# Layer norm by a scaled 16-point matrix in the first stage of a spectral block and feed-forward kernel, on one core

## The chip, the cores and the metric

The kernel runs on one core of one Trainium2 chip. A core has five engines with instruction queues of their own: TensorE (PE in the profile; PEld is its weight loads), VectorE (DVE), ScalarE (ACT), GpSimd (POOL) and SyncE (SP). SP, ACT and POOL also issue the transfers (DMAs). The metric is the device time of one launch in microseconds.

## The reference

x has 2048 rows (tokens) of 448 elements in bf16. Twice over, a spectral block and a feed-forward block are added to it:

```python
x = x + A(layernorm(x), w_r, w_i)      # A: irfft2( rfft2(x) * (w_r + 1j*w_i) ) over tokens and elements
x = x + B(layernorm(x), w1, b1, w2, b2) # B: relu(x @ w1 + b1)**2 @ w2 + b2, inner width 1792
x = x + A(layernorm(x), w_r, w_i)
x = x + B(layernorm(x), w1, b1, w2, b2)
```

The layer norm takes mean and variance of each token's 448 elements and has no weights: (x - mean) / sqrt(var + 1e-5). Both layers use the same weights.

## The kernel before

**Tiling.** x is held as 16 tiles t of 128 partitions by 448 elements; partition p of tile t is token 16p + t. The transform over the 2048 tokens is done as a 16-point one across groups of partitions and a 128-point one behind it; that over the 448 elements is a matrix product (called the d-transform here) with sine and cosine tables that use the symmetry of x[d] and x[447 - d].

**First stage.** For each tile, `ln_stats` gets mean and 1/sqrt(var + eps) (VectorE's batch-norm instructions and ScalarE's root, or for tiles 1 and 3 ScalarE's accumulating square and copy), `norm` (L676) writes the normalised tile into `x_sb`, on GpSimd for 12 tiles and on VectorE for four, and `first_A` multiplies it with the 128x256 matrix `FA_sb` (the 16-point matrix spread over the partitions, and its negative beside it). The normalised tile is the stationary operand, in four matmuls per tile. They leave the sum and the difference of the two halves of the tile, transformed over 16 points, in one bank of PSUM. ScalarE evicts that bank into `XA` (L656). In XA, tiles 0 to 7 take the even columns of the second token index, and tiles 8 to 15 the odd ones, so the d-transform of one half can run when eight tiles are in.

**Spectral block.** Then follow, for each of eight pairs of 16-point outputs: `stage_TD` (d-transform, tables `TD_sb`), `stage_B` (128-point transform, `G_sb`), `stage_W` (the product with w_r and w_i, on VectorE; the weights lie in `Wt`, a half of them copied into reversed order by GpSimd, L657, from two gathered transfers), `stage_Bi` (128-point inverse, `H_sb` and `HS_sb`). `stage_TI` and `stage_AI` go back to elements and tokens.

**Feed-forward block.** `ln_B` squares on ScalarE and sends the tile transposed into `yT`, by matmuls for the first two tiles and by transposing DMAs for the others. `h_part` and `h_pairs` make the inner layer for four tiles at a time, `o_tile` the outer one. In layer 1 each finished tile goes straight into the second spectral block's first stage, `second_A`, which scales `FA_sb` by the tile's 1/deviation (`scaled`, L668) into one of the `NFS` buffers of `Fs`, on VectorE, and uses it as moving operand.

**What sets the order.** Operations are grouped into units, and `ORDER` gives every unit a rank, by tag and place in it ("A1.4" is the first stage for tiles 4 and 5; the letters a, d, p put a unit on ScalarE, VectorE or GpSimd). `ranked` sorts by these, and each engine runs its instructions in that order. `schedule` goes through the sorted units with a cost for each operation. It gives out the eight PSUM banks, and where it expects TensorE to be idle, it puts in matmuls of ones that keep it busy. `emit` puts the waits on semaphores. A queue never looks past an instruction that waits, and SP's queue issues its transfers in rank order as well. Transfers of x go out first, in five pieces:

```python
for i, (a, b) in enumerate(((0, 2), (2, 4), (4, 8), (8, 12), (12, 16))):
    dma("act" if i in (1, 3) else "sp", xin[:, a:b, :], x_dram[:, a:b, :])
```

By the ranks of these five, SP sends tiles 0 to 1, then 12 to 15, then 4 to 7; ACT sends 8 to 11, then 2 and 3, and then FA. On GpSimd, x_sb's padding is zeroed (0.94 us) between the first and second normalisation, and 13 of the 14 copies into `Wt` come after the last one.

Of the kernel before, what the change touches and what calls it, by code (L numbers as in the profile page):

```python
# [15 lines left out]
NFS = 6  # L16
# [6 lines left out]
NB = 8  # L23
# [18 lines left out]
def make_constants():  # L42
# [75 lines left out]
    for g, M in enumerate((cl * np.cos(th), cl * np.sin(th))):  # L118
# [201 lines left out]
class _Sched:  # L320
# [5 lines left out]
    NDSEM = {"sp": 20, "pool": 16, "act": 8, "pe": 0, "dve": 0}  # L326
    DMA_RATE = 400.0
    TURN = (200.0, 100.0)
    SLACK = 40.0
    DMA_SLACK = 100.0  # L330
    BEGIN = 800.0
    WINDOW = 3413.0
# [1051 lines left out]
```

## Time and profile before

| what | value |
|---|---|
| median of three runs | 285.54 us (285.1 to 286.15) |
| the profiled execution | 285.39 us, with a span of 283.6 us from the first instruction to the last |
| TensorE busy, of the span | 263.4 us (93%) |
| VectorE, ScalarE | 209.7 us (74%), 177.9 us (63%) |
| GpSimd | 30.1 us (11%) |
| mean granted TensorE clock | 0.976 |
| moved by DMA | 18.05 MB |

A line of a group reads: line of the kernel, engine, operation, output <- inputs, shapes, count, then busy time in us and the mean of one in ns, then idle time of the engine just before, and what ended most of it. A line of a timeline begins with start and busy length in us. The busy time of matmuls is modelled: their starts are exact, their ends overlap. Many operations are issued by helpers, so a line number is that of the helper: L631 is every matmul, L656 and L657 are evictions and copies on ScalarE and the other engines, L623 every plain transfer.

### The profile page before, as it was taken

To read this page: it belongs to the slowest core of one execution; us is meant where nothing else is said; L and a number is where in the kernel's file an instruction comes from. 1 tells how busy PE (TensorE), PEld (TensorE's weight loads), DVE (VectorE), ACT (ScalarE), POOL (GpSimd) and SP (SyncE) were. 2 spreads that over 40 slices of the span, in tenths; PEclk is the share of its full clock that TensorE was granted. 3 is DMA by queue.
4 is the path that set the end of the run, shared out by engine and by line. 5 is a ranking of instruction groups with operands and counts; after the bars stand their busy time and mean duration, and the time that the engine had idled before them with its cause. 6 is when DMAs were issued, how large, how long until landed. Compare 5 with 4: busy or idle time off the path is not lost.

```text
span 283.6 us, 5727 instructions
## 1 busy us (share of the span) xinstructions
PE 263.4 (93%) x2154; PEld 160.4 (57%) x2156; DVE 209.7 (74%) x669; ACT 177.9 (63%) x389; POOL 30.1 (11%) x35
## 2 busy tenths in 40 slices
PE   7347898999998999999999999999999999999996
PEld 2123666568954455445556876478854454576554
DVE  4643299949968897879699999968879785254732
ACT  3544789789870575778532989598961870987100
POOL 3999900000000000000000000000000000000000
PEclk9875999999999999999999999999999999999999
DMA  7996940001023013230000000002031305400032
GB/s 255 364 361 203 280 168 0 2 0 33 7 40 69 2 37 66 39 38 2 0 2 0 3 2 2 0 0 42 2 75 32 55 0 91 81 10 0 3 113 65
DMA packets 27007, 18.05 MB, mean 64 GB/s; under 512 B 20034, under 2 KB 25378, under 8 KB 26852
## 3 DMA queue, kind: packets, MB, share of 16 engines
q1 hardware_dynamic: 26260, 15.10, 21.0%
q0 software_dynamic: 288, 1.84, 1.7%
q10 hardware_dynamic: 432, 0.75, 0.8%
q8 instruction: 17, 0.28, 0.4%
q14 instruction: 10, 0.08, 0.1%
HBM read 12.18 MB, written 1.84 MB: 49 GB/s over the span
## 4 chain that ended last, share of the span: by engine, by line
PE 81%; POOL 5%; DMA 5%; ACT 4%; DVE 3%; issue 1%; SPq 0%; ACTq 0%; DVEq 0%
PE ps L631 81%; POOL x_sb L676 5%; DMA xin<-in_A_x_dram 3%; ACT arena L656 2%; DMA yT<-arena 2%; ACT tmp L656 1%; DVE st L785 1%; DVE arena L683 1%; DVE x_sb L1084 0%; ACT VT L1108 0%; SPq L623 0%; DVE tmp L683 0%; ACT mv L650 0%; DVE x_sb L1204 0%; DVE mv L776 0%
## 5 line engine op out<-in xcount | busy, mean ns | idle before, releaser
L631 PE MATMUL ps<-yT,W_sb 64*128 64x512 bf16 (+1 forms) x770 | 90.1, 346 | 0.0
L631 PE MATMUL ps<-W_sb,arena 128*128 128x448 bf16 (+1 forms) x476 | 87.8, 342 | 1.2 <-DVE arena L683 1.2
L631 PEld LDWEIGHTS ps<-yT,W_sb 64*128 64x128 bf16 (+1 forms) x770 | 53.4, 95 | 33.9 <-issue 1.5
L650 ACT ACTIVATE arena<-ps,b1col 128x512 bf16<-128x512 f32 x84 | 52.0, 689 | 28.0 <-PE ps L631 27.9
L631 PEld LDWEIGHTS ps<-W_sb,arena 128*128 128x128 bf16 x476 | 45.8, 98 | 38.7 <-DVE arena L683 3.0
L683 DVE TENSOR_TENSOR arena<-arena 128x512 bf16<-128x512 bf16 (+1 forms) x140 | 44.5, 363 | 14.6 <-ACT arena L650 14.5
L656 ACT ACTIVATE XA<-ps 128x512 bf16<-128x512 f32 x32 | 21.9, 743 | 19.4 <-PE ps L631 19.3
L656 ACT ACTIVATE arena<-ps 128x448 bf16<-128x448 f32 (+1 forms) x41 | 24.7, 725 | 3.8 <-PE ps L631 3.6
L1204 DVE SCALAR_TENSOR_TENSOR x_sb<-ps,arena 128x448 bf16<-128x448 f32 (+1 forms) x26 | 15.0, 582 | 13.4 <-PE ps L631 13.2
L1108 ACT ACTIVATE VT<-x_sb 128x448 bf16<-128x448 bf16 x32 | 18.6, 588 | 9.4 <-DVE x_sb L1084 9.4
L631 PE MATMUL ps<-FA_sb,x_sb 128*128 128x256 bf16 x64 | 12.6, 353 | 12.4 <-POOL x_sb L676 7.2
L676 POOL TENSOR_SCALAR x_sb<-xin,mv,rstd 128x448 bf16<-128x448 bf16 x12 | 22.1, 1850 | 3.4 <-DVE rstd L792 3.4
L650 ACT ACTIVATE mv<-mv,epst 128x1 f32<-128x1 f32 (+1 forms) x44 | 12.1, 295 | 12.0 <-DVE mv L786 10.9
L650 ACT ACTIVATE arena<-ps 128x256 bf16<-128x256 f32 x56 | 17.9, 408 | 2.3 <-PE ps L631 2.3
L631 PEld LDWEIGHTS ps<-FA_sb,x_sb 128*128 128x128 bf16 x64 | 6.6, 118 | 18.5 <-POOL x_sb L676 11.3
L656 ACT ACTIVATE VT<-ps 128x512 bf16<-128x512 f32 (+1 forms) x28 | 13.8, 556 | 4.9 <-PE ps L631 4.7
L631 PE MATMUL ps<-yT,VT 64*128 64x512 bf16 x42 | 15.8, 376 | 0.0
L656 ACT ACTIVATE tmp<-ps 128x896 bf16<-128x896 f32 (+1 forms) x20 | 14.4, 793 | 1.2 <-PE ps L631 1.2
L631 PE MATMUL ps<-arena,G_sb 128*128 128x448 bf16 (+1 forms) x76 | 14.5, 333 | 0.7 <-ACT arena L656 0.5
L631 PE MATMUL ps<-HS_sb,arena 128*128 128x512 bf16 x62 | 14.4, 379 | 0.1
L631 PE MATMUL ps<-TD_sb,XA 112*64 112x112 bf16 (+2 forms) x296 | 13.8, 223 | 0.0
L1084 DVE SCALAR_TENSOR_TENSOR x_sb<-ps,mv,xin 128x448 bf16<-128x448 f32 x16 | 10.4, 677 | 4.2 <-PE ps L631 4.2
(71 smaller groups left out, 297.2 us busy)
## 6 DMA issues: line engine op xcount, KB each, us to landing
out_dram<-x_sb SPq DMA_DIRECT2D x15, 112.0 KB, 2.0
W_sb<-in_B_w_dram SPq DMA_DIRECT2D x1, 1568.0 KB, 11.7
W_sb<-in_B_w_dram SPq DMA_DIRECT2D x1, 1344.0 KB, 6.7
HS_sb<-c_HS SPq DMA_DIRECT2D x1, 1024.0 KB, 6.7
G_sb<-c_G SPq DMA_DIRECT2D x1, 960.0 KB, 13.4
xin<-in_A_x_dram SPq DMA_DIRECT2D x2, 448.0 KB, 6.0
xin<-in_A_x_dram ACTq DMA_DIRECT2D x1, 448.0 KB, 4.6
Wt<-in_A_w_r_dram SPq DMA_DIRECT2D x1, 392.0 KB, 14.0
```

The source lines that it names most:

```text
L631: return sch.add("pe", lambda e: e.matmul(_res(o), lhsT, rhs, start=start, stop=stop, skip_group_check=skip), [lhsT, rhs], [o], cost=cost, ...
L650: sch.add("act", lambda e: e.activation(o, _res(i), func, **kw), rd, [o], cost=c)
L656: op = sch.add(engs[0], lambda e: e.activation(o, _res(i), ACT.Copy) if h[0].eng == "act" else e.tensor_copy(o, _res(i)), [i], [o], cost=c ...
L676: op = sch.add(engs[0], lambda e: e.tensor_scalar(o, i, m, r, op0=ALU.subtract, op1=ALU.mult), [i, m, r], [o], cost=c[engs[0]])
L683: sch.add(eng, lambda e: e.tensor_tensor(o, _res(a), b, op), [a, b], [o], cost=_free(o) / rate + 69.0)
L785: small(lambda e, si=si, xi=xi: e.bn_stats(si, xi), [xi], [si], (c1 - c0) / 0.96 + 69.0)
L1084: small(lambda e, xx=xx, xi=xi, r=r, m=m: e.scalar_tensor_tensor(out=xx, in0=_res(r), scalar=m, in1=xi, op0=ALU.subtract, op1=ALU.add), [r ...
L1108: sch.add("act", lambda e, i=i, o=o, x=x: e.activation(o, x, ACT.Square, accum_out=mv[:, i, 4:5]), [x], [o, mv[:, i, 4:5]], cost=560.0)
L1204: small(lambda e: e.scalar_tensor_tensor(out=o, in0=_res(i), scalar=r[0] if r else 1.0, in1=xb[:, t, d0:d1], op0=ALU.mult, op1=ALU.add), [ ...
```

## The change

The tile is not normalised any more. For each tile, `scaled` writes 1/deviation times `FA_sb` (both halves, 128x256) into one of four `Fs` buffers, and the raw tile from `xin` is the stationary operand of the same four matmuls. The mean is taken off in a fifth matmul: `minus` puts -2 x mean (a mean for each half of the tile) into `m2`, in bf16, and a column of it, broadcast to 128 columns, is the stationary operand; the scaled matrix is the moving one, and the result is added to the sums. 13 of the scalings are on GpSimd, those of tiles 8, 14 and 15 on VectorE. x's tiles 0 to 3 come in a transfer each. The feed-forward of the last tile ends in three pieces of columns and not in two. Every unit has a new rank. The planner's margins are larger, and it reckons 1900 ns more for the transposing DMA of tiles 4 and 5 in layer 1.

```diff
-NFS = 6
+NFS = 4
+NORM1 = ()
...
-    SLACK = 40.0
-    DMA_SLACK = 100.0
+    SLACK = 60.0
+    DMA_SLACK = 200.0
...
-        Fs = sb("Fs", [P, NFS, P])
+        Fs = sb("Fs", [P, NFS, 2 * P])
+        m2 = sb("m2", [P, 2, NT])
...
-        for i, (a, b) in enumerate(((0, 2), (2, 4), (4, 8), (8, 12), (12, 16))):
-            dma("act" if i in (1, 3) else "sp", xin[:, a:b, :], x_dram[:, a:b, :])
+        for a, b in ((0, 1), (1, 2), (2, 3), (3, 4), (4, 8), (8, 12), (12, 16)):
+            dma("act" if a in (1, 3, 8) else "sp", xin[:, a:b, :], x_dram[:, a:b, :])
...
+        def minus(a, b):
+            o, i = m2[:, 0, a:b], mv[:, a:b, 0:1].to_broadcast([P, b - a, 2])
+
+            def twice(e):
+                with nc.allow_low_precision(reason="two equal terms"):
+                    return e.tensor_reduce(o, i, mybir.AxisListType.X, ALU.add, negate=True)
+
+            small(twice, [mv[:, a:b, 0]], [o])
...
         def first_A(t):
 
-            xh, m, r = x_sb[:, t, 0:D], mv[:, t, 0:1], rstd[:, t, 0:1]
-            norm(xh, xin[:, t, :], m, r, EV["XH"])
             q = _Tile(1)
-            F2 = FA_sb[:, None, 0:P].to_broadcast([P, 2, P])
+            m, r = mv[:, t, 0:1], rstd[:, t, 0:1]
+            own = t in NORM1
+            if own:
+                x, f = x_sb[:, t, 0:D], FA_sb
+                norm(x, xin[:, t, :], m, r, EV["XN1"])
+            else:
+                x, f = xin[:, t, :], Fs[:, t % NFS, :]
+                scaled(f, FA_sb[:], r, EV["FS"])
+            F2 = f[:, None, 0:P].to_broadcast([P, 2, P])
...
             for k in range(2):
-                mm(o(k), x_sb[:, t, D0[k]:D0[k] + P], F2, k == 0, False, skip=True)
-                mm(o(k), x_sb[:, t, HD + D0[k]:HD + D0[k] + P], FA_sb[:], False, k == 1, skip=True)
+                mm(o(k), x[:, D0[k]:D0[k] + P], F2, k == 0, False, skip=True)
+                mm(o(k), x[:, HD + D0[k]:HD + D0[k] + P], f[:, 0:2 * P], False, own and k == 1, skip=True)
+            if not own:
+                mm(q[lambda b: ps[:, b, :].rearrange("p (k g c) -> p k g c", k=2, g=2)[:, :, 0, :]],
+                   m2[:, 0, t:t + 1].to_broadcast([P, P]), F2, False, True, skip=True)
             A_out(t, q, EV["A1"])
...
-                for d0, d1 in (CUT if t == NT - 1 else ((0, D),)):
+                for d0, d1 in ((0, D),) if t < NT - 1 else CUT_OUT if last else CUT:
...
             ln_stats(g, xin, 0, on_act)
+            minus(g[0], g[-1] + 1)
             for t in g:
                 first_A(t)
```

The ranks of the first stage, and of what is transferred and copied beside it (a unit's number is its place in the order of all engines; in "A1.t" the statistics come first, and the last three of each tile are scaling, matmuls, eviction):

```diff
-    "A1.0": "7 8 11 17 42p 45 48"
-    "A1.2": "83 94 106 131 137d 140 146"
-    "A1.4": "56 75 55 76 85 86 93d 105 108 98p 135 136"
...
+    "sp.xin": "6 4 7 16", "act.xin": "3 10 12", "act.FA_sb": "11"
+    "sp.Wt": "18 17 244 85", "sp.TD_sb": "28", "sp.G_sb": "37 112", "sp.W1_sb": "84 290 291 292", "sp.HS_sb": "111",
+    "sp.TI_sb": "116", "sp.H_sb": "120 119", "sp.b2row": "121", "sp.J_sb": "153", "sp.W2_sb": "288", "pool.x_sb": "183"
+    "A1.0": "9 25 26 30 46 63p 64 65", "A1.1": "13 14 24 23 27 39 43 57 71p 72 78", "A1.2": "8 19 20 32 44 60p 61 62"
+    "A1.3": "38 40 52 41 45 48 49 55 73p 80 81", "A1.4": "31 42 29 33 51 53 56 74p 82 91 77p 93 95"
+    "A1.6": "47 54 34 50 66 67 70 79p 96 104 92p 105 106", "A1.8": "58 68 59 69 83 86 90 89d 107 109 101p 122 128"
+    "A1.10": "75 87 76 88 97 98 100 113p 127 129 123p 130 139"
+    "A1.12": "99 103 94 102 110 114 131 125p 138 143 140p 141 144"
+    "A1.14": "115 118 108 117 132 133 135 136d 145 154 134d 142 151"
+    "TD0.0": "146 148d 155 156a", "TD0.1": "147 149d 157 159a", "TD0.2": "126 137d 158 160d"
+    "M.0": "150 124", "M.1": "187 184", "M.2": "211 152", "M.3": "220 221", "M.4": "248 210"
```

More of the change, by code (lines that the diff above doesn't have):

```diff
@@ L377, in add @@
             u = self.new_unit(eng)
+        if not u.tag:
+            u.tag = f"{eng}.{writes[0].tensor.name}" if writes else eng
         if tile is not None and tile.unit is None:
@@ L477, in schedule @@
                             break
-                        b = min((bank_free[b], b) for b in range(NB) if b not in taken and (
-                            bank_user[b] is None or all(x in done for x in bank_user[b].readers)))
+                        b = min(((bank_free[b], b) for b in range(NB) if b not in taken and (
+                            bank_user[b] is None or all(x in done for x in bank_user[b].readers))), default=None)
+                        if b is None:
+                            break
                         if b[0] > f:
@@ L618, in dma @@
                 fn = lambda e: e.dma_start_transpose(o, i)
-                sch.add(eng, fn, reads, writes, is_dma=True, cost=1000.0, lat=300.0)
+                sch.add(eng, fn, reads, writes, is_dma=True, cost=1000.0, lat=lat)
             else:
@@ L1127, in ln_B @@
                 dma("sp", yT[:, t:t + n, :, :].rearrange("p t k c -> p (t k) c"),
-                    xn[:, 0:n, :].rearrange("p t c -> p (t c)"), transpose=True)
+                    xn[:, 0:n, :].rearrange("p t c -> p (t c)"), transpose=True, lat=1900.0 if t == 4 and not last else 300.0)
             sch.tag = "xb" + sch.tag
@@ L1218, in second_A @@
             A_out(t, q, EV["A2"])
+        CUT_OUT = ((0, HD), (HD, HD + QD), (HD + QD, D))
         CUT = ((0, HD), (HD, D)) if HALVES else ((0, D),)
```

4 lines of the change are left out of this document (2 added, 2 removed), and 187 rows, old and new, of the table ORDER.

## The prediction

> **What bounds the kernel now.** I first read the page's totals and slices: TensorE carries most of the span, and GpSimd's work all lies in the first eighth.
>
> ```profile
> span 283.6 us, 5727 instructions
> PE 263.4 (93%) x2154; PEld 160.4 (57%) x2156; DVE 209.7 (74%) x669; ACT 177.9 (63%) x389; POOL 30.1 (11%) x35
> POOL 3999900000000000000000000000000000000000
> PEclk9875999999999999999999999999999999999999
> L676 POOL TENSOR_SCALAR x_sb<-xin,mv,rstd 128x448 bf16<-128x448 bf16 x12 | 22.1, 1850 | 3.4 <-DVE rstd L792 3.4
> ```
>
> Then the chain of waits in order of time (start, length, what). Up to 30.8 us it runs mostly through GpSimd's normalisations of x (L676).
>
> ```profile
> 1.66 9.08 DMA xin<-in_A_x_dram
> ...
> 17.55 6.13 POOL x_sb L676 x4
> ...
> 24.91 1.85 POOL x_sb L676
> 26.76 0.32 POOL Wt L657
> 27.08 3.70 POOL x_sb L676 x2
> ...
> 30.83 2.63 PE ps L631 x24
> ...
> 33.47 1.32 PE ps L631 x12
> ...
> 34.84 4.35 PE ps L631 x28
> ...
> 39.21 6.53 ACT arena L656 x11
> ```
>
> Third, the timelines of the engines (start, busy length, instructions, idle time before). GpSimd first:
>
> ```profile
> 7.43 1.86 POOL L676 TENSOR_SCALAR x_sb<-xin,mv,rstd 128x448 bf16<-128x448 bf16 x1 [3.35 <-DVE rstd L792]
> 9.24 0.94 POOL L704 MEMSET x_sb<- 128x1024 bf16 x1
> 10.18 16.58 POOL L676 TENSOR_SCALAR x_sb<-xin,mv,rstd 128x448 bf16<-128x448 bf16 x9
> 30.73 4.15 POOL L657 COPY Wt<-yT 128x224 bf16<-128x224 bf16 x13
> ```
>
> GpSimd has no gap from 7.43 us to 34.88. Twelve normalisations at 1.85 us, a memset and a copy fill the time to 30.78; TensorE and ScalarE follow tile by tile:
>
> ```profile
> 11.59 1.86 PE L631 MATMUL ps<-FA_sb,x_sb 128*128 128x256 bf16 x8 [5.19 <-DMA FA_sb<-c_FA]
> 21.30 1.03 PE L631 MATMUL ps<-FA_sb,x_sb 128*128 128x256 bf16 x4 [0.81 <-POOL x_sb L676]
> 30.83 1.48 PE L631 MATMUL ps<-FA_sb,x_sb 128*128 128x256 bf16 x12 [0.80 <-POOL x_sb L676]
> 31.48 1.94 ACT L656 ACTIVATE XA<-ps 128x512 bf16<-128x512 f32 x3 [0.51 <-PE ps L631]
> ```
>
> The last eviction into XA ends at 31.48 + 1.94 = 33.42, and the first G matmul follows at 34.84. From there to the tail the matmuls are nearly dense, so I treat 34.84 us as the marker: whatever it moves, the end moves.
>
> **The first stage, part by part.**
>
> *Scaling instead of normalising.* Removed: 12 GpSimd and 4 VectorE operations on 128x448 with two scalars from memory. Added: 13 GpSimd (letter p in the order) and 3 VectorE operations on 128x256, with one. No row has this form. By size, 1.850 x 256/448 = 1.06 us. The low bound is GpSimd's other one-input operation, the copy:
>
> ```profile
> L657 POOL COPY Wt<-yT 128x224 bf16<-128x224 bf16 x14 | 4.5, 363 | 0.0
> ```
>
> Scaled to 256, 0.363 x 256/224 = 0.41 us. The high bound is an unchanged 1.85. I take 1.06, since operation and engine are those of the 1.85 us row and only the width is new.
>
> The Trainium skill (GPSIMD Engine Reference, Engine selection) calls one-input elementwise work on this engine roughly line-rate; the trace disagrees for the normalisation, 1850 ns for 448 elements being 4.1 ns each. By that rule the scaling would come near the low bound, the second rival's 274.3 us.
>
> *When GpSimd starts.* In the order the first two scalings (tiles 2 and 0, ranks 60 and 63) need reciprocals of ranks 32 and 30, and those stand on VectorE behind the statistics of tiles 5 and 4 (29, 31), so behind x's transfer 4 to 8. That is the third on SP's queue, with two one-tile transfers (224 KB) ahead of it. Its like in the trace is the 448 KB transfer that had 224 KB ahead; VectorE took it up at 7.18 (first row below). The one with 672 KB ahead was taken up at 10.76.
>
> ```profile
> 7.18 0.63 DVE L785 BATCH_NORM_STATS2 st<-xin 128x6 f32<-128x448 bf16 x1
> 10.76 0.63 DVE L785 BATCH_NORM_STATS2 st<-xin 128x6 f32<-128x448 bf16 x1 [2.02 <-DMA xin<-in_A_x_dram]
> 12.11 1.12 DVE L785 BATCH_NORM_STATS2 st<-xin 128x6 f32<-128x448 bf16 x2
> FA_sb<-c_FA ACTq DMA_DIRECT2D x1, 64.0 KB, 9.8
> ```
>
> So 7.2, plus two statistics (1.12) and a reciprocal: 8.4 us, one later than now. Scaling needs FA too, which now lands 9.8 us after its issue (11.6 us), with 672 KB ahead on ACT's queue. It keeps third place there but has 224 KB ahead, so I take it as in by 7.2. Tiles 1 and 3 come through ACT's queue just ahead of it and hold nothing.
>
> *GpSimd's end.* Thirteen scalings and one copy: 8.4 + 13 x 1.06 + 0.32 = 22.5 us, against 30.78. The memset of x_sb (0.94) goes behind the scalings with 12 of the copies, 22.5 + 0.94 + 12 x 0.36 = 27.8 at the latest, against 34.88. Those copies feed the products with Wt; they stay about 7 us earlier, so they are no new limit.
>
> *What follows.* Now 34.84 - 30.78 = 4.06 us lie between GpSimd's end and the marker (matmuls, evictions, 12 d-transform matmuls of the last tiles). These stay; three tiles' fifth matmul adds 3 x 0.11 (twelve matmuls in 1.48 us give 0.11 each behind the first) = 0.3. The early tiles' halves of the d-transform (ranks 126, 146, 147) run under the wait for GpSimd; the halves of tiles 8 to 15 remain, as today 12 matmuls in 1.32. New marker: 22.5 + 4.06 + 0.3 = 26.9, that is 7.9 us earlier.
>
> *Are the other engines fast enough?* A tile costs TensorE five matmuls, at the low clock 5 x 0.2 = 1.0 us (the 1.03 us row for four includes the last one's 0.4 us), at full clock 0.55; ScalarE needs 1.94/3 = 0.65. Both stay under 1.06. VectorE gets ten small reductions that double and negate the means, 0.16 each if they are like its reciprocals (first row below), and three scalings of some 0.3 (the second row is for half the columns). They lie in idle time, since VectorE is busy 3.66 and 3.38 of 6 us in the stretches shown further on; without that cover they would be 2.5 us.
>
> ```profile
> L792 DVE RECIPROCAL rstd<-mv 128x2 f32<-128x2 f32 x6 | 1.0, 164 | 6.2 <-ACT mv L650 6.2
> L668 DVE TENSOR_SCALAR Fs<-FA_sb,rstd 128x128 bf16<-128x128 bf16 x1 | 0.3, 255 | 0.0
> L650 ACT ACTIVATE mv<-mv,epst 128x2 f32<-128x2 f32 x6 | 1.6, 286 | 0.7 <-DVE mv L776 0.4 <-DVE mv L786 0.3
> ```
>
>
> *New waits.* Four Fs buffers mean that the scaling for tile 4 waits for tile 0's matmuls, and so on; GpSimd is then four scalings on, some 4 us, against a matmul group of 1.0, so it doesn't stop. VectorE's scaling of tile 8 (rank 89) waits for tile 4's matmuls: 8.4 + 5 x 1.06 + 1.0 = 14.7. Behind it stand the reciprocal for tiles 10 and 11, and the statistics of 12 to 15. GpSimd wants the first at 8.4 + 9 x 1.06 = 17.9, so there are 3 us to spare. Tile 12's reciprocal, whose root waits on ScalarE behind tile 8's eviction, comes out about even: 0 to 0.5 us, taken as 0. In the second layer the same ring holds its later use, one scaling of 0.25 us per tile; 0, at most one stall of the 0.3 us kind.
>
> **Transfers.** SP now sends the Wt pair ahead of TD and G, and W1 (1344 KB) ahead of HS and H. The DMA engines are full from the start to 20 us (last columns of the stretches: PEclk, DMA share, GB/s):
>
> ```profile
> q0 software_dynamic: 288, 1.84, 1.7%
> ...
> 0.00:8.00 8.00, 5.40 (x16) 1.94 (x16) 4.12 (x12) 2.89 (x7) 3.21 (x9) 1.00 0.77 274
> 8.00:14.00 6.00, 2.15 (x10) 1.24 (x11) 3.66 (x19) 3.18 (x10) 6.00 (x5) 0.79 0.99 352
> 14.00:20.00 6.00, 2.96 (x17) 1.65 (x18) 3.38 (x12) 2.72 (x6) 6.00 (x4) 0.78 1.09 349
> 20.00:26.00 6.00, 3.79 (x17) 1.60 (x15) 1.10 (x6) 2.55 (x5) 6.00 (x4) 0.50 0.86 316
> 43.64 0.60 PE L631 MATMUL ps<-H_sb,arena 128*128 128x256 bf16 x4
> ```
>
> Through G there are 1.8 MB of x, 1.84 MB of gathers (q0), 0.8 of Wt, 0.22 of TD, 0.96 of G and 0.13 of FA and FI, 5.7 MB; at these rates it is in by 18 us, and wanted at 26.9. Through H it is 9.2 MB, in by 29; wanted at 43.64 - 7.9 = 35.7. So they cost nothing; with 7 us less slack either would delay the marker one for one.
>
> **The rest.** The order of all later stages is new too. I know no direction for it: the largest stall it could remove is in the first feed-forward block, 0.28 + 0.94 us, and I bound it by the same size the other way, taken as 0.
>
> ```profile
> 84.83 0.55 PE L631 MATMUL ps<-W_sb,arena 128*128 128x448 bf16 x2 [0.28 <-DVE arena L683]
> 86.32 2.44 PE L631 MATMUL ps<-W_sb,arena 128*128 128x448 bf16 x12 [0.94 <-DVE arena L683]
> 281.10 0.39 DVE L1204 SCALAR_TENSOR_TENSOR x_sb<-ps,arena 128x224 bf16<-128x224 f32 x1 [0.72 <-PE ps L631]
> ```
>
> The last output tile is cut in three, so the closing operation has 112 columns for 224: 0.1 us less. Sum: the profiled execution took 285.39 us (the span of 283.6 and 1.8 around it; the three runs' median is 285.54): 285.4 - 7.9 - 0.1 = **277.4 us**.
>
> **Rivals.**
>
> *The scaling is cheap* (0.41 us). For it: the copy's row. Against it: the normalisation's. GpSimd ends at 14.1, and ScalarE sets the pace: first eviction at 8.4 + 0.4 + 1.2 for the first matmuls = 10.0, sixteen at 0.65 and seven roots at 0.28 (the 286 ns row) to 22.4, and 1.4 for the d-transform: marker 23.8, 11.0 us earlier, 274.3.
>
> *GpSimd starts late, or TensorE stays slow.* If FA lands at 11.6 as today, everything shifts by 3.2: 280.6. For it: FA's 9.8 us; against it: two thirds less ahead of it. If the clock stays at 0.50 (the row 20 to 26) throughout, sixteen tiles at 1.02 from 9.6 on end at 25.9, with 0.74 for the eviction and 1.4 + 0.8 for d-transform matmuls at the low clock the marker is 28.8: 279.3. Against it: the two stretches before show 0.79 and 0.78, though TensorE was busy for less than half of them.
>
> The Trainium skill (TensorE: Matmul & The Clock Gate, Part 1) says that the default is half rate, and that sustained activity over a window of some 3.4 us releases it. The trace agrees as far as the 0.50 and the later 1.00 go; by it half-full TensorE could sit at either, 277.4 or 279.3 us.
>
> *Slower: the scaling's price is per instruction, not per element.* At 1.85 us each GpSimd ends at 8.4 + 13 x 1.85 + 0.32 = 32.8 and the marker comes at 37.2, 2.4 us later: 287.7. It decides from (34.84 - 4.36 - 0.32 - 8.4)/13 = 1.67 us on. Against it: memset and copy on this engine are far shorter, so no fixed cost near a microsecond exists.
>
> *The gain is given back:* later stages lose 8 us by the new order: about 285. Nothing in the profile shows such slack to lose.
>
> **Chances.** Forecast 0.45, cheap scaling 0.20, late or slow 0.23, per instruction 0.07, given back 0.05. Under 0.5% (1.4 us) a measurement here can't tell a change from none. The first three are faster: 0.88; given back is mostly same: 0.04; slower 0.08. The range goes from the cheap case with the stall removed as well (274.3 - 1.2, and a microsecond for ScalarE) to the late one with a loss of 1.2: 272.2 to 282.0.
>
> **What would show it.** The page after should have about 13 GpSimd operations on 128x256 at 1.0 to 1.1 us, beginning at 8.4 and ending by 22.5; evictions into XA done by 25.5; the first G matmul near 27; the same length as now from there. Wrong would be: a mean far from 1.06, FA or x as the first stage's longest wait, a TensorE wait on G, H or Wt, or a stretch behind the marker that is over 1 us longer.

## The result, and the profile after

The kernel after takes 273.74 us (median of four runs, 273.42 to 274.14), beside 285.32 us for the kernel before (four runs, 284.94 to 286.15). The ratio is 0.9591, with a 95% interval of 0.9564 to 0.9618: 11.6 us or 4.1% faster. The forecast of 277.4 us was 3.7 us too long; the range held the time, and the case that came nearest is the rival of a cheap scaling (274.3), though partly by luck, as the last part shows. The profiled execution took 273.45 us with a span of 271.7.

The totals and slices of the page after:

```profile
span 271.7 us, 5828 instructions
PE 259.0 (95%) x2178; PEld 157.6 (58%) x2180; DVE 207.3 (76%) x677; ACT 178.9 (66%) x392; POOL 14.1 (5%) x36
POOL 3268000000000000000000000000000000000000
PEclk9899999999999999999999999999999999999999
```

GpSimd fell from 30.1 us to 14.1, and its work ends in the fourth slice. Its group of scalings after:

```profile
L677 POOL TENSOR_SCALAR Fs<-FA_sb,rstd 128x256 bf16<-128x256 bf16 x13 | 6.1, 478 | 10.3 <-DVE mv L795 7.2 <-PE ps L640 2.8 <-DVE mv L701 0.3
```

One scaling is 478 ns, less than half of the 1.06 us that I took, and GpSimd now waits: 7.2 us for statistics, nearly all of it ahead of its first one, 2.8 us for TensorE to give back one of the four buffers. The chain of waits after shows what took its place:

```profile
1.66 7.89 DMA xin<-in_A_x_dram
9.57 0.63 DVE st L794
10.26 0.52 DVE st L794
11.04 0.49 POOL Fs L677
...
17.62 1.22 ACT XA L665 x2
...
21.43 0.95 DVE Fs L677
...
23.20 1.35 ACT XA L665 x2
24.68 3.97 PE ps L640 x26
```

First comes x's transfer of tiles 4 to 7, which VectorE takes up at 9.57 us and not at 7.2; then ScalarE's evictions into XA; then one VectorE scaling of 0.95 us. On TensorE's timeline after, the first tile, the last d-transform matmuls, the marker (the first G matmul), and the first feed-forward block's outer layer:

```profile
11.67 1.01 PE L640 MATMUL ps<-Fs,xin 128*128 128x256 bf16 x4 [5.52 <-POOL Fs L677]
...
24.68 1.31 PE L640 MATMUL ps<-TD_sb,XA 128*128 128x224 bf16 x12 [0.21 <-ACT XA L665]
25.83 2.43 PE L640 MATMUL ps<-arena,G_sb 128*128 128x448 bf16 x12
...
69.23 5.46 PE L640 MATMUL ps<-W_sb,arena 128*128 128x448 bf16 x28
74.53 0.93 PE L640 MATMUL ps<-tmp,FI_sb 128*128 128x224 bf16 x8
75.30 5.46 PE L640 MATMUL ps<-W_sb,arena 128*128 128x448 bf16 x28
```

The marker moved from 34.84 to 25.83, by 9.0 us. The span fell by 11.9, so the stages behind the marker are 2.9 us shorter too (from the marker to the end 248.8 us before, 245.9 after). One place of that is visible in the rows: the outer layer runs through without the two stalls of 0.28 and 0.94 us that the prediction showed at 84.83 and 86.32.

Three questions were left for the chip: which part of the change earns the first stage's 9 us, why GpSimd's operation is so much cheaper than its size says, and where the 2.9 us behind the marker come from.

### The profile page after: what moved, and what is told of

It is laid out like the page before. It is cut to its first block, busy times and chain, and to the rows that moved or that the text cites. A ratio compares the mean times of both kernels' runs of the same rounds, so it can differ in the third digit from the quotient of the medians.

```text
span 271.7 us, 5828 instructions
## 1 busy us (share of the span) xinstructions
PE 259.0 (95%) x2178; PEld 157.6 (58%) x2180; DVE 207.3 (76%) x677; ACT 178.9 (66%) x392; POOL 14.1 (5%) x36
## 4 chain that ended last, share of the span: by engine, by line
PE 85%; ACT 6%; DVE 3%; DMA 3%; issue 1%; POOL 1%; SPq 0%; ACTq 0%
PE ps L640 85%; ACT arena L665 4%; DMA xin<-in_A_x_dram 3%; ACT XA L665 1%; DVE x_sb L1111 1%; DVE Fs L677 1%; ACT tmp L665 1%; DVE st L794 1%; POOL Fs L677 0%; SPq L632 0%; POOL Wt L666 0%; DVE x_sb L1231 0%; DVE yT L666 0%; DVE tmp L701 0%; DVE tmp L692 0%
## 5 line engine op out<-in xcount | busy, mean ns | idle before, releaser
L640 PE MATMUL ps<-W_sb,arena 128*128 128x448 bf16 (+2 forms) x490 | 87.5, 336 | 0.0
L640 PEld LDWEIGHTS ps<-yT,W_sb 64*128 64x128 bf16 (+1 forms) x770 | 50.7, 95 | 37.2 <-issue 1.7
L659 ACT ACTIVATE arena<-ps,b1col 128x512 bf16<-128x512 f32 x84 | 51.4, 690 | 13.4 <-PE ps L640 13.2
L665 ACT ACTIVATE arena<-ps 128x448 bf16<-128x448 f32 (+1 forms) x42 | 25.6, 727 | 3.3 <-PE ps L640 3.1
L1231 DVE SCALAR_TENSOR_TENSOR x_sb<-ps,arena 128x448 bf16<-128x448 f32 (+2 forms) x27 | 15.1, 566 | 11.9 <-PE ps L640 11.8
L665 ACT ACTIVATE VT<-ps 128x512 bf16<-128x512 f32 (+1 forms) x28 | 14.5, 582 | 4.3 <-PE ps L640 4.2
L640 PE MATMUL ps<-Fs,xin 128*128 128x256 bf16 x64 | 10.2, 296 | 6.1 <-POOL Fs L677 5.5
L640 PEld LDWEIGHTS ps<-TD_sb,XA 112*64 112x64 bf16 (+2 forms) x296 | 12.1, 107 | 2.3 <-ACT XA L665 1.2
L1111 DVE SCALAR_TENSOR_TENSOR x_sb<-ps,mv,x_sb 128x448 bf16<-128x448 f32 x16 | 10.4, 675 | 3.5 <-PE ps L640 3.5
## 6 DMA issues: line engine op xcount, KB each, us to landing
xin<-in_A_x_dram SPq DMA_DIRECT2D x2, 448.0 KB, 11.9
```

The source lines that it names most:

```text
L640: return sch.add("pe", lambda e: e.matmul(_res(o), lhsT, rhs, start=start, stop=stop, skip_group_check=skip), [lhsT, rhs], [o], cost=cost, ...
L659: sch.add("act", lambda e: e.activation(o, _res(i), func, **kw), rd, [o], cost=c)
L665: op = sch.add(engs[0], lambda e: e.activation(o, _res(i), ACT.Copy) if h[0].eng == "act" else e.tensor_copy(o, _res(i)), [i], [o], cost=c ...
L1111: small(lambda e, xx=xx, xi=xi, r=r, m=m: e.scalar_tensor_tensor(out=xx, in0=_res(r), scalar=m, in1=xi, op0=ALU.subtract, op1=ALU.add), [r ...
L1231: small(lambda e: e.scalar_tensor_tensor(out=o, in0=_res(i), scalar=r[0] if r else 1.0, in1=xb[:, t, d0:d1], op0=ALU.mult, op1=ALU.add), [ ...
```

## The experiments

Ratios are to the kernel before, run on the same chip, with their 95% interval. "Marker" is the first G matmul in that kernel's profile.

### Normalising again, all else as after

```diff
-NORM1 = ()
+NORM1 = tuple(range(16))
```

The tiles are normalised on GpSimd (13; a second edit, in `EV`, lets them go there) and VectorE (3), not scaled; the fifth matmul is gone; order and transfers are those of after.

> The changed kernel, with the normalisation of the whole 128x448 tile put back in place of the scaling, on the same engines and in the same order (13 tiles on GpSimd, 3 on VectorE); the transfers of x and all later ranks stay as changed. The fifth matmul is left out, as the normalised tile needs none. Theory (the first stage's gain is GpSimd's time per tile, 0.48 us for 1.85): GpSimd starts at about 11 as in the changed kernel, ends at 11 + 13 x 1.85 + 0.4 = 35.5, and the first G matmul comes 4.1 later, at 39.5 for 25.8: 287.4 us. Rival (the single transfers and the order of the early tiles' d-transform earn most of it): 280 us or less.

Measured: 288.82 us, ratio 1.0121 [1.0102, 1.0141]; marker at 40.91. GpSimd in this kernel:

```profile
L685 POOL TENSOR_SCALAR x_sb<-xin,mv,rstd 128x448 bf16<-128x448 bf16 x13 | 24.0, 1856 | 7.1 <-DVE mv L795 7.1
```

The rest of the change alone makes the kernel 3.5 us slower: without the cheap operation the order of after waits for thirteen times 1.86 us from 11.18 us on. From the marker to the end this kernel takes 247.0 us, 1.1 more than after (245.9); more on this below, where TensorE's fetch is moved.

### Scaling alone, with the order and transfers of before

```diff
-            norm(xh, xin[:, t, :], m, r, EV["XH"])
+            x, f = xin[:, t, :], x_sb[:, t, 0:2 * P]
+            scaled(f, FA_sb[:], r, EV["FS"])
...
+               m2[:, 0, t:t + 1].to_broadcast([P, P]), F2, False, True, skip=True)
```

The scaled matrix is written where the normalised tile was, so there is no ring of four buffers.

> The kernel before, with only the scaling and the fifth matmul put in: old transfers, old order everywhere, old last tile; the scaled matrix goes to the place where the normalised tile was, so there is no ring of four buffers. Theory: FA still lands at 11.6 and sets the start; then TensorE and ScalarE set the pace, 16 tiles at 0.65 and some 1.5 us for the low clock at the start, so the first G matmul comes at 26 to 28 for 34.8, and the rest keeps its old length: 277.6 us (276.5 to 279). Rival (the order and the transfers are needed too): first G matmul at 30 or later, 280.5 us or more.

Measured: 275.3 us, ratio 0.9648 [0.9629, 0.9666]; marker at 26.31. GpSimd's first scaling:

```profile
10.95 0.48 POOL L669 TENSOR_SCALAR x_sb<-FA_sb,rstd 128x256 bf16<-128x256 bf16 x1 [6.88 <-DMA FA_sb<-c_FA]
```

So 10.0 of the 11.6 us come with the scaling alone, 8.5 of them ahead of the marker; the rest lies behind it, where nothing was edited. With before's transfers FA is the last to come, 9.2 us after its issue, which is what the prediction's "late" rival described.

### x in five transfers, all else as after

```diff
-        for a, b in ((0, 1), (1, 2), (2, 3), (3, 4), (4, 8), (8, 12), (12, 16)):
-            dma("act" if a in (1, 3, 8) else "sp", xin[:, a:b, :], x_dram[:, a:b, :])
+        for a, b in ((0, 2), (2, 4), (4, 8), (8, 12), (12, 16)):
+            dma("act" if a in (2, 8) else "sp", xin[:, a:b, :], x_dram[:, a:b, :])
```

> The changed kernel with x in five transfers again (tiles 0 and 1 together on SP, 2 and 3 together on ACT, then FA as third... now second on ACT). Theory: the start is set by the transfer of tiles 4 to 7 and by FA, which have the same bytes ahead of them as before, so the single transfers are worth nothing: 273.7 within 0.7 us. Rival: the early statistics of tiles 0 to 3 matter, and the start comes 1 to 2 us later: 275 us or more.

Measured: 270.38 us, ratio 0.9481 [0.9454, 0.9508]; marker at 22.87. The expectation fell: the single-tile transfers cost 3 us, and undoing them beats the kernel after clearly. In this kernel VectorE takes up tiles 4 to 7 at 6.18 us (after: 9.57), and GpSimd starts 2.4 us earlier:

```profile
6.18 0.62 DVE L794 BATCH_NORM_STATS2 st<-xin 128x6 f32<-128x448 bf16 x1
```

```profile
8.63 1.40 POOL L677 TENSOR_SCALAR Fs<-FA_sb,rstd 128x256 bf16<-128x256 bf16 x3 [4.56 <-DVE mv L795]
```

FA lands 4.9 us after its issue, beside 8.1. The marker comes 3.0 us earlier, more than the 2.4: TensorE's clock doesn't fall here either (its first tile takes 0.60 us behind 2.4 us of idle time; after, 1.01 behind 5.5). In the records of the packets, the two gathers of Wt begin at 5.0 us after and at 6.3 in this kernel. Tiles 4 to 7 go in 128 packets of 3584 bytes, first of that size on SP's queue: by 6 us it has begun 102 of them after, and 130 here. So with seven transfers they run into the gathers, and with five they are nearly through. The number of packets ahead isn't what delays them: those of tiles 0 to 3 (512 after, 256 here) have all begun by 3.6 us after and by 4.1 here. Why the gathers begin earlier with seven transfers isn't shown.

### The gathers sent later

```diff
-            gather(Wm[:, i, :], w.rearrange("(p k) l -> p (k l)", k=16), back[:, 0:1])
+            gather(Wm[:, i, :], w.rearrange("(p k) l -> p (k l)", k=16), back[:, 0:1], [xin[:, 4, :]])
```

After, but GpSimd sends its two gathers only when tiles 4 to 7 are in (the rank of one copy out of them goes back with them).

> The changed kernel with x in seven transfers as it is, but GpSimd's two gathers (1.84 MB) wait until the transfer of tiles 4 to 7 is in, and the first copy that needs them moves behind the scalings (rank 152 for 124). Theory (the single-tile transfers are done early, but the transfer of tiles 4 to 7 and FA behind them then run into the gathers, which take most of the transfer engines from about 6 us on): that transfer is in by about 6.5 us for 9.55, GpSimd starts its scalings at about 9 for 11.0, held by the issue of the gathers, and the first G matmul comes at 24 or earlier: 271.5 us. Rival (the number of transfers ahead in each queue delays it, whatever else runs): it is in after 9 us again, and the gathers only come later: 274 us or more.

Measured: 272.95 us, ratio 0.956 [0.9535, 0.9586]; marker at 26.52. VectorE takes up the tiles at 7.00, and FA lands 5.5 us after its issue, so the gathers were what these two transfers met. No gain is shown (the interval overlaps that of after). GpSimd's queue has the gathers where the first scalings should be:

```profile
9.35 0.94 POOL L708 DMA_INDIRECT yT<-in_A_w_r_dram,back  x1 [0.30 <-DVE m L809]
10.32 1.83 POOL L677 TENSOR_SCALAR Fs<-FA_sb,rstd 128x256 bf16<-128x256 bf16 x4
```

Even so GpSimd starts 0.7 us earlier than after (10.32 for 11.04), and the marker still comes 0.7 later. In this execution TensorE's granted clock is 0.64 of full speed from 8 to 14 us and 0.79 from 14 to 20 (after: 0.74 and 0.97), and the first tile's four matmuls take 1.01 us and those of the next four 1.06 each; after, the fourth is back at 0.60. So the queue and, in this execution, the clock spend what the earlier arrival gains.

### The order of before from the inverse d-transform on

After with its first stage, transfers and first spectral block up to the inverse 128-point transform, but all units from layer 1's inverse d-transform on in the order of before (1000 is added to their numbers, so that they follow), with six buffers for the second layer's scaled matrices and the last tile in two pieces, as before. A few lines stand for all:

```diff
-    "TI0.0": "295 296 297 298 299", "AI0.0": "302 307", "ln0.0": "309 318 326d 312 323 325 328 331d",
+    'TI0.0': '1276 1282 1283 1285 1284',
+    'AI0.0': '1287 1288',
...
```

> The changed kernel, with the ranks from the inverse d-transform of layer 1 on taken from the kernel before, six scaling buffers there and the last tile in two pieces; all ranks up to the inverse 128-point transform of layer 1 stay as changed. Theory (2.9 us of the 11.9 that the span lost are owed to the new order of the later stages, 1.2 of it to the stall in the first feed-forward block that is gone): 273.7 + 2.9 = 276.6 us, and the stall of 0.9 us in front of the outer matmuls is back. Rival (the later stages gain by what the first stage leaves behind, such as transfers that are done earlier): 273.7 to 274.7 us.

Measured: 273.94 us, ratio 0.9593 [0.9564, 0.9622]: the time of after. The outer layer has no stall here either, though its order is the one that stalled before:

```profile
69.47 8.11 PE L761 MATMUL ps<-W_sb,arena 128*128 128x448 bf16 x42
```

So the stall can go without the new order of those stages. In the profiles 0.6 us remain between the two (marker to end 246.5 here, 245.9 after), which the times can't confirm.

### TensorE's instruction fetch moved by 32 instructions

In the records of before, one packet of 16 KB on TensorE's instruction queue, 1.03 us long, starts 1.0 us after the second of the transposing transfers of the first feed-forward block has begun, and that transfer's packets spread over 2.7 us where its siblings' spread over 1.4. In the two experiments above that have before's order there and no stall (scaling alone, and the one just told of), the packet comes 2.0 to 2.4 us ahead of the transfer. The test puts 16 matmuls of ones at TensorE's start, where it is idle, and shifts the fetch by that:

```diff
+                        if first_warm:
+                            for _ in range(16):
+                                w_ = _Op("pe", self.warm_fn(b[1] if isinstance(b, tuple) else b, 128), False, c, 195.0)
...
```

> The kernel before, with 16 more warming matmuls of 128 columns right behind the first one, when TensorE has nothing else to do; nothing else is changed, but each later instruction of TensorE stands 16 matmuls (32 instructions) further on in its code. Theory (later stages of the changed kernel are 1.2 to 1.5 us shorter because TensorE's instruction fetch of 16 KB no longer falls into the transposing transfer of the first feed-forward block): the fetch comes some 3 us earlier, that transfer takes 3.1 us and not 4.6, the stall of 0.28 + 0.94 us near 85 us goes, and the time falls by 1.2 to 1.5 us against the kernel before. Rival (the stall belongs to the order of before, or to the clock): the stall stays and the time is that of before within 0.3 us.

Measured: 284.03 us, ratio 0.9947 [0.9929, 0.9964], 1.4 us less than the 285.46 of before on this chip. The chain of before has this transfer at 4.62 us; the transposing transfers of that stretch in before, then in this kernel, by their median to landing (3.8 is the middle between 4.6 and 3.0); and this kernel's outer layer:

```profile
78.26 4.62 DMA yT<-arena
```

```profile
yT<-arena SPq DMA_TRANSPOSE x2, 3.8
```

```profile
yT<-arena SPq DMA_TRANSPOSE x2, 3.0
```

```profile
79.24 8.11 PE L637 MATMUL ps<-W_sb,arena 128*128 128x448 bf16 x42
```

The packet now starts 2.5 us ahead of the transfer, its packets spread over 1.4 us, and both stalls are gone. Sixteen matmuls that compute nothing make the kernel before faster. So a change of the first stage that alters the number of TensorE's instructions can bring or take 1.4 us in a stage that it doesn't touch, with before's order there.

With after's order the same transfer can be slow and the outer layer doesn't stall. In the kernel after itself the packet (1.4 us long) starts 0.75 us ahead of the transfer, which takes 3.6 us. In the kernel that normalises again (after's order, other instruction count) it falls 1.6 us into the transfer, which takes 4.9 us, longer than in before. The transfer after, then in that kernel, and that kernel's outer layer:

```profile
yT<-arena SPq DMA_TRANSPOSE x1, 3.6
```

```profile
yT<-arena SPq DMA_TRANSPOSE x1, 4.9
```

```profile
84.33 5.46 PE L640 MATMUL ps<-W_sb,arena 128*128 128x448 bf16 x28
89.63 0.93 PE L640 MATMUL ps<-tmp,FI_sb 128*128 128x224 bf16 x8
90.39 5.46 PE L640 MATMUL ps<-W_sb,arena 128*128 128x448 bf16 x28
```

These rows begin 43.4 us behind the marker, as after's do (69.23 - 25.83). So the stall has two cures, each enough by itself: moving the fetch, or the new order, whose planner reckons 1900 ns more for this very transfer. The 1.1 us that the normalising kernel loses behind its marker come later, and their cause is open.

### Which part of the form is dear on GpSimd

After, with GpSimd's 13 scalings in four forms on the same 128x256: a multiplication by r and by a constant; by r and by a second scalar from memory; a subtraction of a scalar from memory and then the multiplication; a subtraction of the constant 0 and then the multiplication. The subtracted and multiplied extras are 0 and 1.

```diff
+                lambda e: e.tensor_scalar(o, i, s, 1.0, op0=ALU.mult, op1=ALU.mult),
+                lambda e: e.tensor_scalar(o, i, s, warm[:, 1:2], op0=ALU.mult, op1=ALU.mult),
+                lambda e: e.tensor_scalar(o, i, warm[:, 2:3], s, op0=ALU.subtract, op1=ALU.mult),
+                lambda e: e.tensor_scalar(o, i, 0.0, s, op0=ALU.subtract, op1=ALU.mult),
```

> The changed kernel with GpSimd's scalings of 128x256 in four forms of the same operation that give the same values: a scalar from memory and the constant 1.0, both multiplied (tiles 0, 4, 12); two scalars from memory, both multiplied (1, 5, 9, 13); a scalar from memory subtracted and one multiplied, as in the normalisation (2, 6, 10); the constant 0.0 subtracted and a scalar from memory multiplied (3, 7, 11). Theory A (the second scalar from memory is what makes the normalisation slow): 0.48, 1.06 or more, 1.06 or more, 0.48 us. Theory B (the subtraction makes it slow): 0.48, 0.48, 1.06, 1.06. Theory C (the width or the tile's place in memory): 0.48 in all four.

Measured (a single run, 274.73 us), the four groups:

```profile
L686 POOL TENSOR_SCALAR Fs<-FA_sb,warm,rstd 128x256 bf16<-128x256 bf16 x3 | 3.7, 1220 | 6.2 <-DVE mv L808 6.2
L687 POOL TENSOR_SCALAR Fs<-FA_sb,rstd 128x256 bf16<-128x256 bf16 x3 | 3.4, 1140 | 0.0
L685 POOL TENSOR_SCALAR Fs<-FA_sb,rstd,warm 128x256 bf16<-128x256 bf16 x4 | 2.2, 550 | 0.6 <-PE ps L640 0.6
L684 POOL TENSOR_SCALAR Fs<-FA_sb,rstd 128x256 bf16<-128x256 bf16 x3 | 1.4, 466 | 0.3 <-PE ps L640 0.3
```

With the subtraction 1.14 and 1.22 us, without it 0.47 and 0.55. A second scalar from memory costs 0.08 us. By size alone the normalisation's 1.85 us scale to 1.06, near the 1.14 and 1.22: my estimate priced the wrong form rightly.

### The kernel before, normalising by a multiplication and an addition

```diff
-            op = sch.add(engs[0], lambda e: e.tensor_scalar(o, i, m, r, op0=ALU.subtract, op1=ALU.mult), [i, m, r], [o],
+            op = sch.add(engs[0], lambda e: e.tensor_scalar(o, i, r, m, op0=ALU.mult, op1=ALU.add), [i, m, r], [o],
...
-            xh, m, r = x_sb[:, t, 0:D], mv[:, t, 0:1], rstd[:, t, 0:1]
+            xh, m, r = x_sb[:, t, 0:D], mv[:, t, 7:8], rstd[:, t, 0:1]
```

One small VectorE operation per group of tiles puts -mean * r into column 7 of `mv`; the planner also puts a few more warming matmuls into the first stage.

> The kernel before, with its normalisation still on GpSimd for 12 tiles and 128x448, but as x * r + (-mean * r), a multiplication and an addition, where it was a subtraction and a multiplication; one more small VectorE operation for each group of tiles makes -mean * r. Theory (the leading subtraction is what makes the form slow on GpSimd): a tile takes 0.65 to 0.85 us instead of 1.85, the first G matmul comes at 26 to 28 us and the time is 276 to 279 us, most of the change's gain without scaling the matrix. Rival (any two-operation form with an addition or subtraction in it is slow, or two scalars from memory on 448 elements are): 1.7 us or more per tile, first G matmul at 34 to 36 us, 285 us.

Measured: 275.61 us, ratio 0.9637 [0.9611, 0.9662]; marker at 25.98. GpSimd's group, and the chain's transposing transfer:

```profile
L676 POOL TENSOR_SCALAR x_sb<-xin,rstd,mv 128x448 bf16<-128x448 bf16 x12 | 8.6, 726 | 7.4 <-DVE mv L1298 5.7 <-DVE mv L776 1.4 <-DVE mv L786 0.2
```

```profile
69.43 4.59 DMA yT<-arena
```

The same tile on the same engine takes 0.73 us instead of 1.85. This is as fast as scaling the matrix with the same order (275.3; the intervals overlap almost wholly), though it still has before's slow transfer: here too the fetch falls 1.0 us into it. The scaled matrix and the fifth matmul earn their gain because the leading subtraction is gone, not because the operand is smaller.

### The memset moved ahead

```diff
-    "pool.x_sb": "183"
+    "pool.x_sb": "37"
```

> The changed kernel, with GpSimd's memset of x_sb's padding moved from among its copies (21.4 us) to right behind the gathers' issue (about 4 us), where GpSimd has nothing to do. Theory (VectorE's last two scalings, 0.95 and 0.75 us for 0.41 of the first, are held up by that memset): all three VectorE scalings take about 0.41 us, TensorE's 0.63 us wait for them shrinks to 0.1 or less, the first G matmul comes 0.5 to 0.8 earlier, 273.1 us. Rival (they are slow for another reason): 0.95 and 0.75 us stay, 273.7 us.

Measured: 273.03 us, ratio 0.9581 [0.9561, 0.9601]; marker at 25.93. VectorE's two last scalings, after (beside GpSimd's memset of 0.95 us from 21.36) and then in this kernel:

```profile
21.43 0.95 DVE L677 TENSOR_SCALAR Fs<-FA_sb,rstd 128x256 bf16<-128x256 bf16 x1
21.70 0.75 DVE L677 TENSOR_SCALAR Fs<-FA_sb,rstd 128x256 bf16<-128x256 bf16 x1
```

```profile
22.00 0.37 DVE L677 TENSOR_SCALAR Fs<-FA_sb,rstd 128x256 bf16<-128x256 bf16 x1
22.35 0.33 DVE L677 TENSOR_SCALAR Fs<-FA_sb,rstd 128x256 bf16<-128x256 bf16 x1
```

The memset does hold VectorE, and the two scalings are 0.4 to 0.6 us shorter without it. The marker doesn't move: ScalarE's evictions, which were next, end as late as they did (24.64 us, after 24.54). ScalarE works without a gap from 16.54 us on (after from 14.60, but for 0.31 us), as TensorE's clock was lower in this execution (0.62 of full speed from 8 to 14 us and 0.81 from 14 to 20; after 0.74 and 0.97). The time's interval overlaps that of after, so no gain is shown, and that 273.0 meets the expected 273.1 is luck. The Trainium skill (SBUF — State Buffer, Who interferes with whom) says that these two engines share a pair of ports, which an instruction of VectorE in a two-port mode, or one of GpSimd, holds to its end. The rows fit that, since both scalings end just after the memset; which mode VectorE was in no run shows.

### The clock kept up

```diff
+                        if first_warm:
+                            for _ in range(22):
+                                w_ = _Op("pe", self.warm_fn(b[1] if isinstance(b, tuple) else b, 512), False, c, 195.0)
...
```

> The changed kernel with 22 more warming matmuls of 512 columns at the start, so that TensorE is idle for less than a microsecond before the first tile instead of 5.5 us. Theory: the clock stays at 1.00, the first tiles take 0.55 us on TensorE instead of 1.06, ScalarE's evictions begin to run one behind another sooner, the first G matmul comes at 24.3 to 24.9 us instead of 25.83 and the time is 0.9 to 1.5 us shorter than the changed kernel's. Rival (GpSimd's scalings from 11.04 us on and ScalarE's queue set the end whatever the clock): first G matmul at 25.6 to 25.9 us and no change of time above 0.3 us.

Measured: 272.46 us, ratio 0.9546 [0.9527, 0.9564], 1.3 us less than after, with intervals that just touch; marker at 23.81. The stretch from 8 to 14 us, after and then here (length, PE, PEld, DVE, ACT and POOL busy, PEclk, DMA share, GB/s):

```profile
8.00:14.00 6.00, 2.33 (x12) 1.64 (x13) 4.29 (x23) 1.62 (x6) 1.87 (x4) 0.74 1.03 395
```

```profile
8.00:14.00 6.00, 6.00 (x43) 3.86 (x41) 5.04 (x28) 3.36 (x10) 3.01 (x7) 1.00 1.03 387
```

The marker came 2.0 us earlier, more than forecast, but 1.0 of it isn't the clock's: in this execution tiles 4 to 7 were taken up at 8.58, and GpSimd started at 10.05 instead of 11.04. The clock's share is then about 1 us, an estimate from these two numbers.

### Putting the findings together

```diff
-    "dve.warm": "0", "dve.epst": "5", "act.warm": "193", "act.FA_sb": "11", "sp.xin": "6 4 7 16",
-    "act.xin": "3 10 12", "pool.ones": "21", "pool.back": "22", "pool.yT": "36 35", "pool.x_sb": "183",
+    "dve.warm": "0", "dve.epst": "5", "act.warm": "13", "act.FA_sb": "2", "sp.xin": "4 7 16",
+    "act.xin": "3 12", "pool.ones": "21", "pool.back": "22", "pool.yT": "36 35", "pool.x_sb": "37",
...
-    "M.5": "188 235", "M.6": "224 223", "dve.arena": "2", "sp.J_sb": "153", "sp.TD_sb": "28", "sp.G_sb": "37 112",
+    "M.5": "188 235", "M.6": "224 223", "dve.arena": "2", "sp.J_sb": "153", "sp.TD_sb": "16", "sp.G_sb": "37 112",
```

After with x in five transfers, FA first on ACT's queue, a root as ScalarE's first operation (one table load, where after has two of 1.28 us), TD ahead of Wt, and the memset early.

> The changed kernel with five edits of the order that the traces point to: x in five transfers; FA ahead of x's transfers on ACT's queue; ScalarE's root on a constant first, so that one table is loaded and not two; TD ahead of the Wt pair on SP's queue (TensorE waited 1.45 us for it with five transfers); GpSimd's memset early. Theory: with five transfers the first reciprocal waited for ScalarE at 7.7; without the second table load (1.28 us) GpSimd starts at about 7.4 for 8.63, and the memset is worth another 0.5: first G matmul at 21 to 21.8 for 22.87, 268.7 us (268 to 269.5). Rival (by then ScalarE's evictions or x's last tiles set the pace): 270.0 us or more.

Measured: 269.44 us, ratio 0.946 [0.9438, 0.9483]; marker at 21.85. It beats both kernels; against the five transfers alone (0.9481) the intervals overlap, so what the other edits add is not settled. On TensorE's timeline:

```profile
9.17 0.60 PE L640 MATMUL ps<-Fs,xin 128*128 128x256 bf16 x4 [2.04 <-POOL Fs L677]
```

The first tile's matmuls take 0.60 us, where they took 1.01 after: TensorE was idle for 2.0 us and not 5.5, and the clock never fell. GpSimd starts at 8.54 and not at the 7.4 expected, as it waits for VectorE's statistics. ScalarE then evicts without a gap from 9.91 to 20.56 us.

### Four of those evictions on VectorE

The kernel just told of, with a letter d at the evictions of tiles 7, 9, 12 and 15; the planner puts four warming matmuls (1.03 us) in TensorE's idle time.

```diff
-    "A1.6": "47 54 34 50 66 67 70 79p 96 104 92p 105 106", "A1.8": "58 68 59 69 83 86 90 89d 107 109 101p 122 128",
+    "A1.6": "47 54 34 50 66 67 70 79p 96 104 92p 105 106d", "A1.8": "58 68 59 69 83 86 90 89d 107 109 101p 122 128d",
...
-    "A1.14": "115 118 108 117 132 133 135 136d 145 154 134d 142 151", "TD0.0": "146 148d 155 156a",
+    "A1.14": "115 118 108 117 132 133 135 136d 145 154 134d 142 151d", "TD0.0": "146 148d 155 156a",
```

> The kernel is the one with five transfers of x, FA first on ACT's queue and one table load, and four of the first stage's sixteen evictions into XA (tiles 7, 9, 12 and 15) go from ScalarE to VectorE; four warming matmuls of 512 columns also stand between d-transform matmuls. Theory: there ScalarE evicts without a gap from 9.91 to 20.56 us and sets the pace, so with four evictions of 0.65 us fewer the first G matmul comes at 20.0 to 20.5 us instead of 21.85 and the time is 267.5 to 268.5 us. Rival: TensorE's 0.545 us per tile or the last scalings set the pace anyway, or VectorE's evictions hold up its statistics: no gain, 269.4 us and the first G matmul at 21.5 us or later.

Measured: 271.07 us, ratio 0.9491 [0.9474, 0.9509]; marker at 23.51, 1.7 us later than without it. The rival held: there is no gain (the times' intervals overlap, so a loss isn't clear). TensorE's two waits, and what VectorE did ahead of the last one:

```profile
15.97 0.54 PE L640 MATMUL ps<-TD_sb,XA 128*128 128x224 bf16 x4 [0.91 <-DVE XA L666]
...
22.36 1.31 PE L640 MATMUL ps<-TD_sb,XA 128*128 128x224 bf16 x12 [0.74 <-DVE XA L666]
```

```profile
20.41 1.20 DVE L666 CAST arena<-ps 128x448 bf16<-128x448 f32 x2 [0.25 <-PE ps L640]
21.50 0.71 DVE L666 CAST XA<-ps 128x512 bf16<-128x512 f32 x1
```

The last eviction now stands on VectorE behind two evictions of the d-transform. ScalarE was relieved of 2.6 us, but the d-transform waits for whichever engine is last, and in this order that became VectorE. Another order of VectorE's queue was not tried.

## Why the prediction was right, and where it was wrong

**Mechanism.** Right: GpSimd's normalisation bounded the first stage, and what the marker gains the end gains. Eight kernels with after's later stages have 245.8 to 245.9 us from marker to end, with markers between 21.85 and 27.04; the ninth, which normalises again, has 247.0 with its marker at 40.91.

**Scaling instead of normalising.** The step that failed is the choice of 1.06 us, "since operation and engine are those of the 1.85 us row and only the width is new". The operation was not the same: the normalisation leads with a subtraction. 0.478 us stands near the low bound of 0.41, and the mechanism of the cheap-scaling rival, ScalarE setting the pace, is what the chain shows once GpSimd has begun. I had its best evidence in hand, the copy's row, and gave it 0.20.

The Trainium skill (GPSIMD Engine Reference, Engine selection) has one-input work on this engine roughly line-rate. The runs agree for multiplications (0.47 us for 256 elements, beside VectorE's 0.33 to 0.37 for the same shape; 0.73 for 448 with an addition) and disagree for the subtraction (1.14 to 1.22 for 256, 1.85 for 448). In the prediction I let the dear form speak for all.

**When GpSimd starts.** Forecast 8.4, measured 11.04. The part that failed is the arrival of tiles 4 to 7 and of FA by 7.2, which I read off transfers with the same number of bytes ahead of them. Bytes were the wrong measure: the same bytes in five transfers arrive in time and in seven they meet the gathers. The "late" rival had the right place and nearly the size (3.2 us forecast, 2.6 measured), but FA alone as the cause; tiles 4 to 7 were as late.

**GpSimd's end, and what follows.** Forecast 22.5 and 26.9; measured 20.79 (19.86 + 0.93) and 25.83. That these are close is luck, as the errors mostly took each other away: 13 x 0.58 = 7.6 us less work, 2.6 us later start, 2.8 us of waits for buffers and 0.5 of other waits. The cheap-scaling rival's sum with the measured start gives 11.04 + 0.4 + 1.2 + 16 x 0.65 + 7 x 0.28 + 1.4 = 26.4, the nearest of all cases. That its 274.3 came so near the time is luck too: its marker of 23.8 was 2.0 us early, and the 2.9 us by which the later stages got shorter were not in it.

**New waits.** "so it doesn't stop", said of GpSimd at the ring of four buffers, was wrong at 0.478 us a scaling, but TensorE waited for GpSimd only once, before the first tile, so it cost nothing. VectorE's three scalings were not all hidden in idle time: that a memset on GpSimd would stretch two of them by 1 us together was not foreseen, and 0.63 us of TensorE's idle time came from it; a gain in the time from moving it is not shown.

**The clock.** Forecast as a rival of 1.9 us; it was 0.74 of full speed from 8 to 14 us and cost about 1 us, by the estimate above. The Trainium skill (TensorE: Matmul & The Clock Gate, Part 1) has the clock fall after an idle window of some 3.4 us; the runs agree, with 1.01 us for the first tile's matmuls behind 3.6, 4.4 and 5.5 us of idle time in three kernels, 0.71 and 0.76 behind 4.8 and 5.0 in two, and 0.60 behind 2.0 and 2.4 us.

**Transfers.** Right for Wt, TD and G: no TensorE wait on them at the marker. Wrong for x and FA, as said.

**The rest.** Taken as 0 within 1.2 us, measured -2.9. The stall that I named as the largest removable piece did go. Shifting the fetch alone removes it, and the new order does without it, as the 4.9 us transfer without a stall shows; so its going can't be credited to one of the two alone. Shifting the fetch in the kernel before shortens its span behind the marker by 1.6 us, and by 1.4 in the times. With after's first stage and first spectral block, and before's order behind them, 0.7 us more are gone. Of these, 0.4 lie between the marker and the first matmul of the inverse d-transform, 22.8 us in that kernel and in after for 23.2 in before and with the fetch shifted, so in the block whose order is the new one. The new order of the stages behind adds 0.6 in the profiles; for this and the other 0.3 there is no cause shown. The tail's closing operation fell from 0.39 to 0.27 us, as the 0.1 forecast.

## What to carry to other kernels

Price an operation by its form on its engine, not only by its width: here the same normalisation written as a multiplication and an addition took 0.73 us instead of 1.85, and that rewriting was worth 9.8 us of the change's 11.6. When an order is changed, judge the stages that it doesn't touch by where instruction fetches fall before crediting the order, and when forecasting an arrival, look at what other queues have in flight by then, not only at the bytes ahead in its own. An engine freed of its bound hands it on at once: here to x's arrival, ScalarE's evictions and VectorE's queue in turn, so a further step can earn nothing (the memset) or move the marker back (the evictions shared).

## What the runs showed of the hardware that was not expected

- GpSimd: subtraction first, then multiplication, 1.14 to 1.22 us on 128x256; two multiplications 0.47 to 0.55 us. Whether an addition in first place, or a subtraction in second, is dear as well was not run.
- A GpSimd memset of 0.95 us stretched VectorE's scalings from 0.37 and 0.33 us to 0.95 and 0.75.
- A 16 KB instruction packet of about 1 us inside a transposing transfer took it from 3.0 to 4.6 us in two kernels and to 4.9 in a third; starting 0.75 us ahead of it, to 3.6 in one; 2 us ahead of it, it cost nothing in three.
- Four transfers of one tile instead of two of two tiles delayed the next transfer (taken up at 9.57 us instead of 6.18; at 8.58 in another kernel with the four) and the time by 3 us. Holding back two gathers brought it to 7.00.
